# Attention pooling and a two-layer squared-ReLU block: a list planner with other durations, engine choice for the rounding, joined PSUM reads and 120-row token tiles

## The chip, the cores and the metric

The kernel runs on one core of a Trainium2 chip. The metric is device time in microseconds (us) of one execution; lower is better. A core has a matrix engine (PE, with its weight loads shown apart as PEld), a vector engine (DVE), a scalar engine (ACT), a general engine (POOL) and a queue engine (SP) that issues transfers. Each runs its own instruction list in order. A matrix product lands in PSUM, here eight banks of 512 float32 columns on 128 partitions; POOL doesn't read PSUM in this kernel.

## The reference

```python
def _attn_ref(x, inducing):            # x: 4 x 12480 x 128, inducing: 32 x 128
    ...
    def mab(q, kv):
        s = scale * (q @ kv.transpose(0, 2, 1))
        s = s - s.max(-1, keepdims=True)
        a = np.exp(s)
        a /= a.sum(-1, keepdims=True) + 1e-09
        return a @ kv
    h = mab(I, x)
    return mab(x, h)

def _moe_ref(x, w_in, w_out):          # 128 -> 2048 -> 128
    h = x @ w_in
    g = np.where(h >= 1, h, np.where(h <= -1, 0.0, (h + 1) ** 2 / 4))
    return g @ w_out
```

For each of four batches the 32 inducing rows attend over all 12480 tokens, then all tokens attend over the 32 summaries, and the 49920 results go through the two-layer block. The weights arrive as float64.

## The kernel before, in words

Tokens are cut into chunks of 480, 26 to a batch, 104 in all; four chunks are a group, seven groups a batch. Four kinds of work are listed as operations with an engine, a cost, a lag, a due time and buffers, and a planner sorts them:

- `load_in` and `load_out` fetch the weights in eight pieces each and turn float64 bits into float32 with six short DVE steps (`mag_bits`, `to_single`, `shift`, `upper`, `weight`, `lower`) and a POOL addition (`join`). A piece of `w_out` whose index is in `ROUND` is split into a rounded part `w_hi` and a rest `w_lo`; the other two stay whole (`w_f`).
- `summarize(b)` is the first attention. Per chunk it loads tokens as rows (`xn`: 96 partitions with 5 tokens each) and in columns (`xT`; in batch 0 by PE transposes and an ACT copy, L373, later by transfers and a DVE transpose, L388). Per group it makes scores (L407), maxima (L412), exponentials `e1` (ACT, L418), transposes them on PE (L439), copies them out to `eN` (L445, L446) and weighs the rows (L452). A chain `c1` to `c12` then folds the groups into `hT`, and `hw` is `hT` times the first weights (L556 to L566). So the first layer becomes one product of attention weights `aT` with `hw`.
- `attend(b, g)` is the second attention of a group: scores (L591), a DVE transpose, maximum, difference, exponential, sum (L614), the 1e-9 and the reciprocal (`invert`, L617 and L618), a product on POOL (`norm`), a transpose back, rounding on ACT and a rest on POOL (L632). Transfers then copy the result into `aT`. For the very first group POOL's two steps run on DVE (`hasty`).
- `chunk(b, c)` has eight steps k, 832 over the run, and is most of the work. Each step makes two products h (PE, L680), each with a bank of its own; two ACT instructions write max(h+1, 0) into the two halves of `w` (`rise`, L688, from here on the relu); one ACT instruction squares both halves (L695); two DVE instructions form min(max(h, 1), w) (`bound`, L701, the clamp). Six steps of eight are then rounded into `hi` (on the engine that `ROUND` names: four times DVE L716, once POOL L711, once ACT L713), POOL forms `lo = w - hi` (L719), and PE adds three products per half into the one bank `o` (L744). The other two steps add w in full float32. At a chunk's end DVE transposes `o` into `oT` (L754) and SP stores it.

The planner (`Plan.order`) walks time forward. When an engine is free it takes, among the operations whose inputs and buffers are ready by the listed costs and lags, the one with the earliest due time. Buffers are pools of slots (`SLOTS`): seven banks `h`, one bank `o`, eight `w`, four `hi`, four `lo`. A bank of the pool `h` is taken when a product is issued and given back after the clamp. The program that results is a fixed list per engine; on the chip semaphores alone decide when a row runs. So costs, lags and due times set the order and nothing else:

```python
ROUND = {0: "DVE", 1: "POOL", 3: "DVE", 4: "DVE", 6: "ACT", 7: "DVE"}
BEHIND = dict(h=-2600, r=-2000, s=-1000, t=0, hi=1200, lo=2400, p=7000, ps=12000)
...
if op.due < best.due:
```

Of the kernel before, what the change touches and what calls it, by code (L numbers as in the profile page):

```python
# [17 lines left out]
ROUND = {0: "DVE", 1: "POOL", 3: "DVE", 4: "DVE", 6: "ACT", 7: "DVE"}  # L18
# [6 lines left out]
BEHIND = dict(h=-2600, r=-2000, s=-1000, t=0, hi=1200, lo=2400, p=7000, ps=12000)  # L25

LEAD = 60000
# [5 lines left out]

class Slot:


    def __init__(self, pool, turn=None):
        self.pool, self.left, self.until, self.place, self.tile = pool, 0, 0, None, None
        self.turn = turn


class Op:


    def __init__(self, engine, cost, lag, due, emit, needs, uses):
        self.engine, self.cost, self.lag, self.due, self.emit = engine, cost, lag, due, emit
        self.uses = uses
        self.start = self.after = 0
        self.unmet, self.then = 0, []
        for n in needs:  # L50
            n.then.append(self)
            self.unmet += 1
        for s in self.uses:
            s.left += 1


class Plan:
# [5 lines left out]
    def add(self, engine, cost, lag, due, emit, needs=(), uses=()):  # L63
        op = Op(engine, cost, lag, due, emit, [n for n in needs if n], uses)
        self.ops.append(op)
        return op

    def order(self):
        engines = sorted({op.engine for op in self.ops})
        free = dict.fromkeys(engines, 0)  # L70
        able = {e: [] for e in engines}
        for op in self.ops:
            if not op.unmet:
                able[op.engine].append(op)
        spare = {p: [(0, i) for i in range(n)] for p, n in SLOTS.items()}
        turn = dict.fromkeys(SLOTS, 0)
        now, done = 0, []
        while len(done) < len(self.ops):
            later = []
            took = False  # L80
            for e in engines:
# [3 lines left out]
                best = None  # L85
                for op in able[e]:
                    at = op.after
                    opens = {}
                    for s in op.uses:
                        if s.place is None:  # L90
                            if s.turn not in (None, turn[s.pool]):
# [6 lines left out]
                    elif best is None or op.due < best.due:  # L98
                        best = op
# [3 lines left out]
                able[e].remove(best)  # L103
                best.start = now
                done.append(best)
                free[e] = now + best.cost
                later.append(free[e])
                for s in best.uses:
                    if s.place is None:
                        got = min(spare[s.pool])  # L110
                        spare[s.pool].remove(got)
                        s.place = got[1]
                        if s.turn is not None:
                            turn[s.pool] += 1
                seen = now + best.lag
                for s in best.uses:
                    s.left -= 1
                    s.until = max(s.until, seen)
                    if not s.left:
                        spare[s.pool].append((s.until, s.place))  # L120
                for n in best.then:
                    n.unmet -= 1
                    n.after = max(n.after, seen)
                    if not n.unmet:
                        able[n.engine].append(n)
# [7 lines left out]
def attn_moe(  # L133
# [14 lines left out]
    T = 5  # L148
    TP = 96
    CW = T * TP  # L150
    NB = CW // M
    R = TP // M
# [6 lines left out]
    assert NCH * CW == N and Q * M == P and C == P and R * M == TP and R * T == NB  # L159
# [6 lines left out]
    x_rows = x.rearrange("b (k p t) c -> b k p t c", p=TP, t=T)  # L166
# [4 lines left out]
        h=([P, 512], F32), o=([P, 512], F32), xn=([TP, T, C], F32), xT=([C, CW], F32),  # L171
        xr=([C, NB, M], F32), e1=([P, CW], F32), eN=([TP, T, P], F32), hw=([P, 512], F32R),
        w=([P, 2, CW], F32), hi=([P, 2, CW], F32R), lo=([P, 2, CW], F32R), aT=([P, CW], F32R),
        s2=([P, NB, M], F32), a=([P, CW], F32), ahi=([P, CW], F32R), oT=([C, NB, M], F32),
    )
    count = [0]

    def make(slot, shape=None, dtype=None):

        count[0] += 1  # L180
        where = psum if slot.pool in ("h", "o") else work
        s, d = FORM[slot.pool]
        slot.tile = where.tile(
# [12 lines left out]
    def in_turn(pool):  # L196
        turns[pool] += 1
        return Slot(pool, turns[pool] - 1)
# [46 lines left out]
    def load_f32(src, due, dst=None):  # L245
# [17 lines left out]

        def mag_bits():
# [5 lines left out]
        def to_single():  # L270

            nc.vector.tensor_scalar(
# [542 lines left out]
```

## Time and profile before

| what | value |
|---|---|
| median of 3 runs | 1832.63 us (1831.53 to 1833.14) |
| the profiled execution's own time | 1832.42 us |
| span in its trace | 1830.6 us |
| PE busy | 1736.9 us (95%) |
| DVE busy | 1714.6 us (94%) |
| ACT busy | 1724.2 us (94%) |
| POOL busy | 1579.0 us (86%) |

Around the span lie 1.8 us. Busy time counts an engine as busy while at least one instruction is under way, so with instructions that overlap in the pipeline a busy engine can still have room. What an instruction really costs in a full stretch is read from the distance of the starts in the timeline. PE's busy time has modelled ends. The share of 16 transfer engines in use is 0.28 by the page, so transfers don't fill theirs.

### The profile page before, as it was taken

What the parts mean: (1) busy time and instruction counts of PE and PEld (TensorE: products, weight loads), DVE (VectorE), ACT (ScalarE), POOL (GpSimd) and SP (SyncE); (2) the same over time, 40 slices, a digit from 0 to 9 for tenths busy, and PEclk for the clock granted to TensorE, in tenths of its full rate; (3) what the DMA queues carried; (4) which work ended last, traced back from release to release, by engine and by line L of the source; (5) the groups of instructions that cost most, each with busy time, mean ns of one, the idle gap of its engine ahead of it and who ended that gap; (6) DMA issues with size and microseconds to landing.
All of it is one profiled execution on the core that took longest, in us unless ns stands there. A gap on an engine that the chain in (4) does not pass through costs nothing.

```text
span 1830.6 us, 26794 instructions
## 1 busy us (share of the span) xinstructions
PE 1736.9 (95%) x8075; PEld 1235.7 (67%) x8075; DVE 1714.6 (94%) x2715; ACT 1724.2 (94%) x2807; POOL 1579.0 (86%) x810
## 2 busy tenths in 40 slices
PE   8699999999989999999999999999999999999998
PEld 5367767666667766767766766666676676677776
DVE  5999999999899999999999999999999999999997
ACT  7499999999989999999989999999998999999997
POOL 1499899888789989988978898898897999999997
PEclk9699999999999999999999999999999999999999
DMA  8532333222223333332223323332211111111111
GB/s 233 97 57 57 67 63 69 48 62 59 40 52 58 65 60 74 63 76 38 50 41 62 73 58 57 64 71 48 36 26 30 31 33 33 33 34 27 35 31 17
DMA packets 395200, 101.84 MB, mean 56 GB/s; under 512 B 369680, under 2 KB 383024, under 8 KB 395056
## 3 DMA queue, kind: packets, MB, share of 16 engines
q1 hardware_dynamic: 394960, 100.02, 28.1%
q8 instruction: 64, 1.05, 0.2%
q14 instruction: 80, 0.66, 0.1%
q10 hardware_dynamic: 96, 0.12, 0.0%
HBM read 48.94 MB, written 25.56 MB: 41 GB/s over the span
## 4 chain that ended last, share of the span: by engine, by line
PE 52%; ACT 21%; DVE 19%; issue 5%; DMA 1%; SPq 1%; POOL 0%; DVEq 0%; POOLq 0%; ACTq 0%
PE o L744 36%; PE h L680 10%; ACT w L688 10%; ACT w L695 9%; DVE w L701 8%; DVE hi L716 4%; DVE oT L754 3%; DVE sm L617 1%; PE h L452 1%; ACT hi L713 1%; PE h L591 1%; PE h L407 1%; PE h L439 1%; DMA xn<-in_x 1%; PE h L556 1%
## 5 line engine op out<-in xcount | busy, mean ns | idle before, releaser
L719 POOL TENSOR_TENSOR lo<-w,hi 128x960 fp32r<-128x960 f32 x624 | 1404.3, 2269 | 181.6 <-ACT hi L713 63.9
L701 DVE SCALAR_TENSOR_TENSOR w<-h,w 128x480 f32<-128x480 f32 x1664 | 991.8, 644 | 50.8 <-ACT w L695 48.8
L688 ACT ACTIVATE w<-h 128x480 f32<-128x480 f32 x1664 | 913.4, 627 | 50.8 <-PE h L680 48.1
L695 ACT ACTIVATE w<-w 128x960 f32<-128x960 f32 x832 | 888.2, 1068 | 3.0
L680 PE MATMUL h<-aT,hw 128*128 128x480 f32 x1664 | 639.1, 438 | 26.8 <-DVE w L701 10.1
L744 PE MATMUL o<-hi,w_hi 128*128 128x480 f32 x1248 | 496.6, 398 | 0.0
L716 DVE TENSOR_REDUCE hi<-w 128x960 fp32r<-128x960 f32 x416 | 472.1, 1135 | 16.6 <-PE o L744 1.6
L744 PE MATMUL o<-lo,w_hi 128*128 128x480 f32 x1248 | 473.5, 379 | 0.4 <-POOL lo L719 0.4
L744 PE MATMUL o<-hi,w_lo 128*128 128x480 f32 x1248 | 473.8, 380 | 0.0
L680 PEld LDWEIGHTS h<-aT,hw 128*128 128x128 f32 x1664 | 312.0, 189 | 210.2 <-DVE w L701 96.2
L744 PE MATMUL o<-w,w_f 128*128 128x480 f32 x832 | 388.2, 578 | 41.8 <-DVE oT L754 37.2
L744 PEld LDWEIGHTS o<-hi,w_hi 128*128 128x128 f32 x1248 | 234.5, 188 | 57.0 <-issue 25.1
L744 PEld LDWEIGHTS o<-hi,w_lo 128*128 128x128 f32 x1248 | 234.3, 188 | 46.9 <-issue 12.0
L744 PEld LDWEIGHTS o<-lo,w_hi 128*128 128x128 f32 x1248 | 234.1, 188 | 37.9 <-POOL lo L719 1.1
L744 PEld LDWEIGHTS o<-w,w_f 128*128 128x128 f32 x832 | 149.1, 190 | 161.5 <-issue 75.5
L713 ACT CAST hi<-w 128x960 fp32r<-128x960 f32 x104 | 107.2, 1031 | 5.2 <-DVE w L701 5.2
L711 POOL TENSOR_SCALAR hi<-w 128x960 fp32r<-128x960 f32 x104 | 104.4, 1004 | 0.0
L754 DVE STREAM_TRANSPOSE oT<-o 128x480 f32<-128x480 f32 x104 | 69.7, 670 | 8.9 <-PE o L744 7.6
L388 DVE STREAM_TRANSPOSE xT<-xr 128x480 f32<-128x480 f32 x78 | 51.8, 664 | 1.0 <-DMA xr<-in_x 1.0
L304 POOL TENSOR_TENSOR w_in_sb<-hi,lo 128x256 f32<-128x256 f32 x8 | 6.0, 755 | 36.3 <-DVE hi L294 36.3
L452 PE MATMUL h<-xn,eN 96*32 96x128 f32 x930 | 36.3, 275 | 0.5 <-ACT eN L445 0.5
L632 POOL TENSOR_TENSOR a<-a,ahi 128x480 fp32r<-128x480 f32 (+1 forms) x27 | 33.1, 1226 | 1.6 <-ACT ahi L629 1.6
(83 smaller groups left out, 616.8 us busy)
## 6 DMA issues: line engine op xcount, KB each, us to landing
out<-oT SPq DMA_DIRECT2D x416, 60.0 KB, 2.2
xn<-in_x SPq DMA_DIRECT2D x93, 240.0 KB, 3.9
xr<-in_x SPq DMA_DIRECT2D x312, 60.0 KB, 2.5
aT<-ahi SPq DMA_DIRECT2D x208, 60.0 KB, 2.0
aT<-a SPq DMA_DIRECT2D x206, 60.0 KB, 2.0
w<-in_x SPq DMA_DIRECT2D x11, 240.0 KB, 4.5
w<-in_moe_w_in SPq DMA_DIRECT2D x8, 256.0 KB, 5.3
w<-in_moe_w_out SPq DMA_DIRECT2D x8, 256.0 KB, 6.0
```

The costliest lines, as they stand in the source:

```text
L388: nc.vector.transpose(make(xT[b, c]), xr.tile.rearrange("c n i -> c (n i)"))
L452: nc.tensor.matmul(p[q * M : (q + 1) * M, :C], eN[g].tile[:, t, q * M : (q + 1) * M], xn[g * Q + q].tile[:, t, :], start=(t == 0), stop=(t ...
L680: nc.tensor.matmul(make(h)[:, :CW], hw[b][ft // 4].tile[:, ft % 4 * P : (ft % 4 + 1) * P], aT[b, c].tile, start=True, stop=True,)
L688: nc.scalar.activation(w.tile[:, i], h.tile[:, :CW], AF.Relu, bias=1.0)
L695: nc.scalar.activation(w.tile, w.tile, AF.Square, scale=0.5)
L701: nc.vector.scalar_tensor_tensor(w.tile[:, i], h.tile[:, :CW], 1.0, w.tile[:, i], op0=ALU.max, op1=ALU.min)
L711: nc.gpsimd.tensor_scalar(make(hi), w.tile, 1.0, 0.0, op0=ALU.mult, op1=ALU.add)
L713: nc.scalar.copy(make(hi), w.tile)
L716: nc.vector.tensor_reduce(make(hi), w.tile.unsqueeze(3), axis=AX.X, op=ALU.max)
L719: nc.gpsimd.tensor_sub(make(lo), w.tile, hi.tile.bitcast(F32))
L744: nc.tensor.matmul(acc.tile[:, :CW], wt, g, start=(first and n == 0), stop=(last and n == len(terms) - 1),)
L754: nc.vector.transpose(make(oT).rearrange("c n i -> c (n i)"), acc.tile[:, :CW])
```

## The change

- The planner's costs and lags are replaced by other numbers, and it knows three more things: on the same engine a result is usable a fixed time (`RAW`) after the cost; an operation may list several engines with a cost, lag and due time for each; and PE pays `RETILE` when it changes between products that use the whole array and products that use part of it. `KEEP` is 0, so that last rule doesn't move the choice.
- The rounding into `hi` lists DVE, ACT and POOL, with later due times for ACT and POOL, in place of a fixed engine for each k. The batches' `eN` copies list DVE and ACT.
- All eight banks are one PSUM tile, `banks`, and a slot is a number in it. If the two products of a step stand in an even bank and the next, and both are ready, the two relus become one instruction over 960 columns, and likewise the two clamps.
- Batches 1 to 3 load rows as 4 tokens for each of 120 partitions, 480 pieces of 512 bytes in place of 96 of 2560, so the exponentials are transposed in 4 pieces, not 5, fill one bank, and one copy makes `eN`. `e1` and `xT` are written in order and read in strides, where before both the read and the write were strided.
- `to_single` and `join` of `w_out` run on POOL, `join` of `w_in` on DVE; the middle of the `w_out` conversion waits for batch 0's `hT`, and `load_out` is listed after `summarize(0)`.
- The 1e-9 of `attend` moves from DVE to POOL (`guard`).
- Of the three terms of a split product, the one with `w_lo` is issued first.

In the program that comes out, 169 of 832 relu pairs and 249 of 832 clamp pairs are joined. Roundings on DVE go from 416 to 384, on ACT from 104 to 99, on POOL from 104 to 141. DVE has 18 full `eN` copies less of each of two kinds and 10 of the new kind; ACT has 8 of the new kind more. Products in the weighing step go from 520 to 442. POOL gains 28 guards.

The core of the diff:

```diff
-ROUND = {0: "DVE", 1: "POOL", 3: "DVE", 4: "DVE", 6: "ACT", 7: "DVE"}
+SPLIT = (0, 1, 3, 4, 6, 7)
...
-BEHIND = dict(h=-2600, r=-2000, s=-1000, t=0, hi=1200, lo=2400, p=7000, ps=12000)
+BEHIND = {
+    "h": -4400, "r": -3050, "s": -500, "t": 400, "hi": 3300, "hi ACT": 1900, "hi POOL": 9600,
+    "lo": 2200, "p": 9300, "ps": 8900,
+}
+RAW = dict(DVE=205, ACT=130, POOL=100, PE=100, SP=0)
...
+    def pick(self, spare, now):
+        free = {i for t, i in spare if t <= now}
+        if self.near and self.near.place is not None and self.near.place ^ 1 in free:
+            return self.near.place ^ 1
+        if self.first:
+            return min(free, key=lambda i: (i ^ 1 not in free, i % 2, i))
+        return min(free, key=lambda i: (i ^ 1 in free, i))
...
+    def beside(self):
+        a, b = self.uses[0].place, self.twin.uses[0].place
+        return a % 2 == 0 and b == a + 1
...
+                if best.merged and best.beside():
+                    other = best.twin
+                    if other in able[e] and other.ready(e) <= now:
...
-    x_rows = x.rearrange("b (k p t) c -> b k p t c", p=TP, t=T)
+    x_rows = x.rearrange("b (k t p) c -> b k p t c", p=120, t=4)
...
+        spare = nc.vector if first else nc.gpsimd
...
-        v = add("DVE", 340, 470, due, upper, [v], [raw, top])
+        v = add("DVE", 360, 500, due, upper, [v, after], [raw, top])
...
+        def guard():
+            nc.gpsimd.tensor_scalar(sm[:rows], sm[:rows], 1e-9, None, op0=ALU.add)
         def invert():
-            nc.vector.tensor_scalar(sm[:rows], sm[:rows], 1e-9, None, op0=ALU.add)
             nc.vector.reciprocal(sm[:rows], sm[:rows])
...
+    def each(of, i, hs_, w, do):
+        if of[1 - i].wide:
+            return
+        if of[i].wide:
+            do(w.tile, banks[:, hs_[0].place : hs_[0].place + 2, :CW])
+        else:
+            do(w.tile[:, i], hs_[i].tile[:, :CW])
...
-                u = add(ROUND[k], cost, lag, due + BEHIND["hi"], upper, ts, [hi, w])
+                ways = dict(
+                    DVE=(1058, 1285, at), ACT=(884, 1065, at + BEHIND["hi ACT"]),
+                    POOL=(1085, 1180, at + BEHIND["hi POOL"]),
+                )
+                u = add(ways, 0, 0, at, lambda upper=upper, by=by: upper(by=by), ts, [hi, w])
...
                         terms = [
+                            (w_lo[k][:, i, :], hi.tile[:, i, :]),
                             (w_hi[k][:, i, :], hi.tile[:, i, :]),
-                            (w_lo[k][:, i, :], hi.tile[:, i, :]),
                             (w_hi[k][:, i, :], lo.tile[:, i, :]),
```

DVE in the start, from the first step of batch 0's chain (`m_0`, L489 before and L568 after, is `c1`). Before, conversions of `w_out` (L266 to L294) stand between the steps of the chain:

```order
L489 TENSOR_REDUCE m_0_94<-mg 128x1
L283 SCALAR_TENSOR_TENSOR lo_898<-w_802,lo_898 128x256
L266 TENSOR_SCALAR hi_910<-w_811 128x256
L495 TENSOR_REDUCE mrow_95<-h_907 1x128
L289 TENSOR_SCALAR hi_889<-lo_898 128x256
L272 TENSOR_SCALAR hi_910<-hi_910 128x256
L294 SCALAR_TENSOR_TENSOR hi_889<-w_802,hi_889 128x256
L507 TENSOR_SCALAR nm_96<-h_916 128x1
```

The same place after:

```order
L568 TENSOR_REDUCE m_0_81<-mg 128x1
L574 TENSOR_REDUCE mrow_82<-banks 1x128
L586 TENSOR_SCALAR nm_83<-banks 128x1
L592 TENSOR_TENSOR fs_84<-banks,sg 128x7
L593 TENSOR_REDUCE tot_85<-fs_84 128x1
L599 TENSOR_SCALAR rs_86<-banks 128x1
L600 RECIPROCAL rs_86<-rs_86 128x1
L603 SCALAR_TENSOR_TENSOR ff<-banks,rs_86,fold 128x224
L615 COPY hT_859<-banks 128x128
L351 SCALAR_TENSOR_TENSOR lo_775<-w_652,lo_775 128x256
```

The conversions moved behind `hT` (L536 before, L615 after).

DVE at the end of a chunk in the middle of the run, from the transpose of `o`. Before, clamps are 480 wide, one by one (L701), and L716 is the rounding:

```order
L754 STREAM_TRANSPOSE oT_8451<-o_8235 128x480
L716 TENSOR_REDUCE hi_8455<-w_8387 128x960
L701 SCALAR_TENSOR_TENSOR w_8418<-h_8392,w_8418 128x480
L701 SCALAR_TENSOR_TENSOR w_8418<-h_8412,w_8418 128x480
L701 SCALAR_TENSOR_TENSOR w_8435<-h_8416,w_8435 128x480
L716 TENSOR_REDUCE hi_8482<-w_8418 128x960
L701 SCALAR_TENSOR_TENSOR w_8435<-h_8422,w_8435 128x480
```

After, at the same transpose (L855; L788 is the clamp, L811 the rounding):

```order
L855 STREAM_TRANSPOSE oT_7384<-banks 128x480
L788 SCALAR_TENSOR_TENSOR w_7323<-banks,w_7323 128x480
L811 TENSOR_REDUCE hi_7396<-w_7309 128x960
L788 SCALAR_TENSOR_TENSOR w_7369<-banks,w_7369 128x960
L788 SCALAR_TENSOR_TENSOR w_7388<-banks,w_7388 128x480 x2
L788 SCALAR_TENSOR_TENSOR w_7398<-banks,w_7398 128x480 x2
L811 TENSOR_REDUCE hi_7443<-w_7388 128x960
L811 TENSOR_REDUCE hi_7452<-w_7398 128x960
```

One clamp of this piece is joined, and roundings stand further behind their clamps.

POOL in the first chunks, where L711 (after: L806) is a rounding and L719 (after: L814) forms `lo`. Before, a rounding stands ahead of its own `lo`, once in eight steps:

```order
L711 TENSOR_SCALAR hi_1499<-w_1427 128x960
L719 TENSOR_TENSOR lo_1510<-w_1427,hi_1499 128x960
L719 TENSOR_TENSOR lo_1534<-w_1459,hi_1519 128x960
L719 TENSOR_TENSOR lo_1566<-w_1479,hi_1549 128x960
L719 TENSOR_TENSOR lo_1594<-w_1517,hi_1582 128x960
L719 TENSOR_TENSOR lo_1617<-w_1538,hi_1602 128x960
```

After:

```order
L806 TENSOR_SCALAR hi_1389<-w_1322 128x960
L806 TENSOR_SCALAR hi_1403<-w_1338 128x960
L814 TENSOR_TENSOR lo_1415<-w_1322,hi_1389 128x960
L814 TENSOR_TENSOR lo_1440<-w_1338,hi_1403 128x960
L806 TENSOR_SCALAR hi_1462<-w_1393 128x960
L814 TENSOR_TENSOR lo_1476<-w_1374,hi_1449 128x960
```

Roundings come in bunches there, and a `lo` of an older step can stand behind a rounding of a newer one.

More of the change, by code (lines that the diff above doesn't have):

```diff
@@ L102, in order @@
                 took = True
[L103 to L107, printed above, removed]
+                for x in best.choice:
+                    able[x].remove(best)
+                cost, lag, _ = best.choice[e]
                 for s in best.uses:
                     if s.place is None:
[L110 to L114, printed above, removed]
@@ L115, in order @@
-                seen = now + best.lag
-                for s in best.uses:
+                        s.place = s.pick(spare[s.pool], now)
+                        spare[s.pool] = [x for x in spare[s.pool] if x[1] != s.place]
+                        turn[s.pool] += s.turn is not None
+                both = [best]
+                if best.merged and best.beside():
+                    other = best.twin
+                    if other in able[e] and other.ready(e) <= now:
+                        able[e].remove(other)
+                        both.append(other)
+                        best.wide = True
+                        cost, lag = best.merged
@@ L117, in order @@
+                if e == "PE" and best.tiled != tiled:
+                    cost, lag, tiled = cost + RETILE, lag + RETILE, best.tiled
+                for op in both:
+                    op.start, op.engine, op.cost, op.lag = now, e, 0, lag
+                    done.append(op)
+                best.cost = cost
+                free[e] = now + cost
+                later.append(free[e])
+                for s in [s for op in both for s in op.uses]:
                     s.left -= 1
-                    s.until = max(s.until, seen)
+                    s.until = max(s.until, now + lag)
@@ L175, in attn_moe @@
     )
+    banks = psum.tile([P, SLOTS["h"] + SLOTS["o"], 512], F32, name="banks")
     count = [0]
@@ L180, in make @@
         count[0] += 1
-        where = psum if slot.pool in ("h", "o") else work
+        if slot.pool in ("h", "o"):
+            slot.tile = banks[:, slot.place + (SLOTS["h"] if slot.pool == "o" else 0), :]
+            return slot.tile
         s, d = FORM[slot.pool]
-        slot.tile = where.tile(
+        slot.tile = work.tile(
             shape or s, dtype or d, tag=f"{slot.pool}{slot.place}", name=f"{slot.pool}_{count[0]}"
@@ L672, in chunk, with square @@
             w = in_turn("w")
[L673 to L676 removed]
+            h0 = in_turn("h")
+            hs_ = [h0, in_turn("h", h0)]
+            ms, rs_, ts = [], [], []
+            def square(w=w):
+                nc.scalar.activation(w.tile, w.tile, AF.Square, scale=0.5)
+            for i, h in enumerate(hs_):
                 def hidden(k=k, i=i, h=h):
@@ L694, in square @@
-            def square(w=w):
-                nc.scalar.activation(w.tile, w.tile, AF.Square, scale=0.5)
-            s = add("ACT", 896, 1036, due + BEHIND["s"], square, ss, [w])
-            for i in range(2):
-                def bound(i=i, h=hs_[i], w=w):
-                    nc.vector.scalar_tensor_tensor(
-                        w.tile[:, i], h.tile[:, :CW], 1.0, w.tile[:, i], op0=ALU.max, op1=ALU.min
-                    )
-                ts.append(add("DVE", 565, 700, due + BEHIND["t"] + i, bound, [s], [hs_[i], w]))
```

223 lines of the change are left out of this document (134 added, 89 removed).

## Prediction

> **What bounds the kernel now.** I read, in this order, busy time by stretch, the chain of work that ended last, the waits, and the timeline for the distance of starts. First the page's span and the stretch from 77 us (just after the first relu) to the last transpose; its columns are start and end, length, then busy time (and count) of PE, PEld, DVE, ACT, POOL, then clock, share of transfers and GB/s. Then the chain from 120 to 1790 us by engine and line.
>
> ```profile
> span 1830.6 us, 26794 instructions
> 77.00:1825.00 1748.00, 1683.95 (x7545) 1202.01 (x7544) 1661.97 (x2568) 1681.36 (x2731) 1561.20 (x783) 1.00 0.27 50
> by line: PE o L744 38.1%; PE h L680 10.6%; ACT w L688 10.4%; ACT w L695 9.5%; DVE w L701 8.5%; issue 5.4%; DVE hi L716 4.1%; DVE oT L754 2.7%; DVE sm L617 1.3%; ACT hi L713 1.2%; PE h L591 1.1%; PE h L452 1.1%; PE h L407 0.7%; PE h L439 0.5
> ```
>
> No engine bounds this alone. In 1748 us PE idles 64, ACT 67, DVE 86, POOL 187, and the chain passes through PE, ACT and DVE in turn. POOL hardly stands in it. The clock is full. What costs time is that in-order engines wait for each other; who waits for DVE says most (idle of PE before h and before o, us and times, and the two rows of ACT and DVE):
>
> ```profile
>   DVE w L701: 106.3, 323
>   DVE oT L754: 48.9, 92
>   POOL lo L719: 1.5, 3
> ACT w L688 <- PE h L680: 48.1, 76, 1.7
> DVE w L701 <- ACT w L695: 48.8, 102, 1.5
> L719 POOL TENSOR_TENSOR lo<-w,hi 128x960 fp32r<-128x960 f32 x624 | 1404.3, 2269 | 181.6 <-ACT hi L713 63.9 <-DVE hi L716 61.1 <-PE h L680 19.8
> ```
>
> PE waits 106.3 us for clamps to give banks back and 48.9 us for `o` to be transposed, 155 us of waiting for DVE (loads and products both counted). Then ACT waits 48.1 us for PE's h. For `lo` PE waits only 1.5 us: POOL's 181.6 us of idle are slack today.
>
> **The change part by part.** True prices, from distances of starts (start, length, engine, instructions):
>
> ```profile
> 1019.18 1.08 ACT L688 ACTIVATE w<-h 128x480 f32<-128x480 f32 x2
> 1020.08 1.08 ACT L695 ACTIVATE w<-w 128x960 f32<-128x960 f32 x1
> 1020.98 1.10 ACT L688 ACTIVATE w<-h 128x480 f32<-128x480 f32 x2
> 1028.62 1.14 ACT L713 CAST hi<-w 128x960 fp32r<-128x960 f32 x1
> 1029.50 1.17 ACT L695 ACTIVATE w<-w 128x960 f32<-128x960 f32 x1
> 1023.80 1.78 DVE L701 SCALAR_TENSOR_TENSOR w<-h,w 128x480 f32<-128x480 f32 x3
> 1025.49 1.14 DVE L716 TENSOR_REDUCE hi<-w 128x960 fp32r<-128x960 f32 x1
> 1026.55 3.12 DVE L701 SCALAR_TENSOR_TENSOR w<-h,w 128x480 f32<-128x480 f32 x5
> 1004.21 0.99 POOL L711 TENSOR_SCALAR hi<-w 128x960 fp32r<-128x960 f32 x1
> 1005.17 1.21 POOL L632 TENSOR_TENSOR a<-a,ahi 128x480 fp32r<-128x480 f32 x1
> ```
>
> A relu pair takes 0.90, a square 0.90, an ACT rounding 0.88; three clamps take 1.69, so a pair 1.13; a DVE rounding 1.06, a POOL rounding 0.96.
>
> *DVE's load.* 32 roundings fewer: 32 x 1.06 = 34 us. Joined clamps: no such instruction ran; the nearest of 960 columns is the rounding, 1.06, so 249 x (1.13 - 1.06) = 17 us (bounds: 0, and 249 x 0.56 = 139 if the second half cost nothing, which the equal ACT rows for 2 x 480 and 960 columns speak against). For the guard and `eN`, and for what else is priced below:
>
> ```profile
> L617 DVE TENSOR_SCALAR sm<-sm x28: 160/916/2090, 68.6 to 1742.5; 128x15 f32<-128x15 f32 x24, 64x15 f32<-64x15 f32 x4
> L617 DVE TENSOR_SCALAR sm<-sm 128x15 f32<-128x15 f32 x24 | 24.4, 1018 | 0.0
> L445 DVE COPY eN<-h 96x512 f32<-96x512 f32 x18 | 12.1, 675 | 0.0
> L446 DVE COPY eN<-h 96x128 f32<-96x128 f32 x18 | 4.9, 275 | 0.0
> L418 ACT ACTIVATE e<-h,nb 128x480 f32<-128x480 f32 x24 | 22.9, 954 | 0.0
> L611 ACT ACTIVATE s<-s 128x480 f32<-128x480 f32 x24 | 15.2, 634 | 3.0 <-DVE s L606 3.0
> L373 ACT COPY xT<-h 128x480 f32<-128x480 f32 x26 | 24.8, 1071 | 6.9 <-PE h L368 6.9
> L629 ACT CAST ahi<-a 128x480 fp32r<-128x480 f32 x24 | 15.4, 643 | 0.3 <-DVE a L626 0.3
> L452 PE MATMUL h<-xn,eN 96*32 96x128 f32 x930 | 36.3, 275 | 0.5 <-ACT eN L445 0.5
> L439 PE MATMUL h<-ident,e 128*96 128x128 f32 x120 | 17.9, 276 | 3.1 <-DVE w L701 2.2 <-ACT e L418 0.7
> ```
>
> The guard touches 15 columns and takes 0.16 to 2.09 us: a fixed small work and a stall up to the length of one POOL `lo` (2.27). Off DVE it frees some 27 us, and by the chain (1.3% of 1670) 22 of them lie on the path. On POOL it costs 28 x 0.16 = 4 us. `eN` gives back 12.1 + 4.9 - 10 x 0.675 = 10 us, with the half-sized copies some 12. Together 34 + 17 + 27 + 12 = 90 us, and DVE's busy time falls from 1662 to 1572.
>
> *What that is worth.* At least the 22 us on the chain, at most all 90. Between them I scale PE's wait with DVE's ratio of busy to idle time, an assumption of mine and not a reading: 1662/86 = 19 before; with a stretch of some 1700, 1572/128 = 12, a third less. A third of PE's 155 us is **52 us**, my value; it lies between the ends, and the row it rests on (106.3 and 48.9) is the wait that I think ends last.
>
> *ACT.* 5 roundings fewer: -4. Joined relus: 169 x (0.90 - 0.90) is 0 by the nearest row, the square; at most 169 x 0.45 = 76, for which nothing speaks; I take 0. 8 `eN` copies more, at DVE's 0.675: +5. The exponentials L418 lose one strided side: between 0 and 21 x (0.954 - 0.634) = 7; half, -3. Net **-2**.
>
> *PE.* For 21 groups 4 of 20 weighing products and one of 5 transposes go: 78 products are two records each, 36.3/930 x 2 x 78 = 6, and 21 x 17.9/120 = 3. Half of PE's time is on the chain: **-4**. `w_lo` first issues the same products: 0, since its third term still waits for `lo`, as before. One `banks` tile: dependences still go by bank: 0.
>
> *POOL.* 37 roundings x 0.96 = 36, guards 4, so 40 us more; today they would fit into 187 us of idle. But a rounding ahead of a `lo` makes that one 0.96 later, and behind `lo` wait PE's products, the `hi` and `lo` slots and the end of the chunk. From 0 (hidden) to 40; a third, **+13**, since idle shrinks to about 100.
>
> *Start.* The last copy of a group's sum (a row of the timeline), then pieces of the chain (start, length, what):
>
> ```profile
> 48.44 0.25 ACT L459 COPY hs<-h 64x128 f32<-64x128 f32 x1
> 50.50 0.15 DVE m L489
> 50.98 0.73 DVE hi L266
> 53.34 0.73 DVE hi L266
> 54.67 0.73 DVE hi L272
> 59.57 0.30 DVE hT L536
> 79.41 0.64 DVE w L701
> ```
>
> `c1` starts 1.8 us after its last input (48.69), and three conversions of 0.73 stand in the chain to `hT`: up to 1.8 + 2.2 = 4 us earlier without them. `xT` copies become like L629: 26 x (1.071 - 0.643) = 11 us less ACT work in the start, of which I count 3, as PE and transfers alternate with ACT there. But the conversions come back between `hT` and the first clamp, where DVE is busy: some 15 more of 0.2 to 0.3 us, +4, against attention steps of later groups put off. Net **-3**, between -9 and +4. On POOL `to_single` and `join` meet an idle engine there.
>
> *Transfers.* 480 pieces per chunk of rows:
>
> ```profile
> xn<-in_x SPq DMA_DIRECT2D x93, 240.0 KB, 3.9
> xr<-in_x SPq DMA_DIRECT2D x312, 60.0 KB, 2.5
> ```
>
> `xr` moves 480 small pieces in 2.5 us already. Even if 78 loads took twice 3.9 us each, nine slots and a group per 3.3 chunks (over 50 us) cover them; without that cover it would be 78 x 3.9 = 304 us. SP has the same 1263 issues: 0.
>
> *Sum.* 1830.6 - 52 - 2 - 4 + 13 - 3 = 1782.6 us of span; with the 1.8 us around it 1784.4, and the median shown lies 0.2 above the profiled execution's 1832.42: **1784.6**.
>
> The Trainium skill, "Perfetto Trace Analysis", section "Optimizing Scalar/DVE Operations", gives a DVE instruction about 125 ns of fixed access time on PSUM and an ACT one about 51 ns. By that, an estimate from that page, joined clamps would save 31 us, not 17, and joined relus 9, not 0, and the sum would be some 15 us lower. The two equal ACT rows here (0.90) disagree for ACT, and the sum stays with them.
>
> **Rivals.**
> - *More gain (about 1759).* ACT's own work by starts is 832 x 1.80 + 104 x 0.88 = 1590 and some 55 of smaller things, 1645 in 1748. If the new order keeps ACT at 98% of its starts, the stretch is about 1677 ((1645 - 2)/0.98), the span 1830.6 - 71 - 3, and 2 around it: 1758.6. For it: all waits named above end at DVE. Against: PE, ACT and POOL would all be above 95%.
> - *Waits move (about 1815).* Only the chain's 22 us come back, ACT, PE and the start give 9, and POOL takes 13: 1830.6 - 18 + 1.8. For it: ACT and PE were as idle as 67 and 64 us, so something else may end next.
> - *Joining holds banks (about 1810).* A joined clamp gives its first bank back 0.56 us later. PE waited before 323 of 1664 products; 249 x 0.56 x 323/1664 = 27 us. The same section says that breaking instructions up may let work finish sooner where the engine isn't full but makes others idle, which is this rule against the change; the trace shows the bank wait but no joined instruction.
> - *POOL decides, slower (about 1870).* If POOL's idle time isn't slack but the latency of rounding into `lo`, it stays: 1561 + 40 + 187 = 1788 in place of 1748, +40, less 3. For it: POOL's idle ends 61.1 us at DVE's and 63.9 at ACT's rounding, and bunched POOL roundings lengthen that way. Against: only 1.5 us of PE's waits end at `lo`. It decides once POOL's idle stays above some 150 us.
> - *No change (1829 to 1836).* The order is no better in sum: the later due times of the rounding eat what DVE gives.
>
> **Chances.** Forecast (1765 to 1804) 0.45, more gain 0.13, waits move 0.16, joining 0.09, POOL slower 0.12, no change 0.05. A measurement of this kernel tells some 0.2% (about 4 us) from no change. Faster 0.83, same 0.05, slower 0.12. The range 1748 to 1828 leaves out the slower cases and the low tail.
>
> **What would show it.** Right: DVE's busy time 1600 to 1640 us in all, waits of PE's h for the clamp near 70 us and of o for the transpose near 35, the guard at about 0.2 us on POOL or stalled there at no one's cost, POOL's idle before `lo` near 100. A joined clamp's start-to-start distance of 1.06, a joined relu's 0.90. `hT` at 55 to 56 us and the first clamp at 75 to 79. Wrong: PE waiting tens of us for `lo` (POOL), unchanged waits for clamps with 960-wide clamps ending them (joining), or ACT idle before h unchanged.

## The result and the profile after

The changed kernel takes 1785.14 us (median of 4 runs, 1782.57 to 1786.76) beside 1832.42 for the kernel before: a ratio of 0.9741, 95% interval 0.9724 to 0.9758, or 47.5 us less. The forecast was 1784.6. Executions at a lower clock are left out of all ratios: one of the four of s6 below (3136.64 us at a granted clock of 0.83) and one of the kernel before (1940.1 us at 0.85).

The total came out as forecast, but not by the route it was given. First the page's span and busy times, then the stretch from 70 us to the last transpose (start and end, length, busy time of PE, PEld, DVE, ACT, POOL, clock, transfers, GB/s; the first relu is at 75.7):

```profile
span 1784.7 us, 25996 instructions
PE 1718.4 (96%) x7898; PEld 1231.5 (69%) x7898; DVE 1636.2 (92%) x2376; ACT 1693.5 (95%) x2642; POOL 1619.7 (91%) x875
70.00:1779.00 1709.00, 1665.80 (x7373) 1197.51 (x7369) 1596.58 (x2263) 1663.93 (x2572) 1611.35 (x860) 0.99 0.28 52
```

In this stretch PE idles 43 us, ACT 45, POOL 98 and DVE 112 (before, in 1748 us: 64, 67, 187, 86). DVE now has more slack than POOL. The waits (who waits, for whom: us, times, longest) and the group of `lo`:

```profile
PEld banks L775 <- DVE w L788: 98.3, 255, 4.7
PE banks L775 <- DVE w L788: 14.6, 18, 4.2
PEld banks L845 <- DVE oT L855: 33.2, 66, 1.3
PE banks L845 <- DVE oT L855: 13.8, 32, 1.2
PEld banks L845 <- ACT w L783: 7.5, 13, 1.6
PEld banks L845 <- ACT w L769: 5.8, 14, 0.6
PEld banks L845 <- POOL lo L814: 3.3, 6, 1.1
ACT w L783 <- PE banks L775: 21.2, 36, 1.5
L814 POOL TENSOR_TENSOR lo<-w,hi 128x960 fp32r<-128x960 f32 x624 | 1400.0, 2271 | 68.9 <-DVE hi L811 22.5 <-ACT hi L808 12.6 <-PE banks L775 9.0
```

PE's waits for clamps are 112.9 us (106.3 before) and for the transposed `o` 47.0 (48.9 before). The waits that the forecast cut by a third did not fall. These two rows of the kernel before did, from 66.7 us to the 13.3 of the fifth and sixth row above:

```profile
PEld o L744 <- ACT w L688: 42.9, 53, 1.8
PEld o L744 <- ACT w L695: 23.8, 35, 2.2
```

The stretch from the first clamp to the last one is 50 us shorter; the start, up to the first clamp, is 4.5 us longer. The clamp's line in the changed kernel, then in the kernel before:

```profile
L788 DVE SCALAR_TENSOR_TENSOR w<-banks,w x1415: 586/647/1159, 83.9 to 1772.2; 128x480 f32<-128x480 f32 x144, 128x960 f32<-128x960 f32 x33
```

```profile
L701 DVE SCALAR_TENSOR_TENSOR w<-h,w x1664: 584/646/664, 79.4 to 1818.0; 128x480 f32<-128x480 f32 x185
```

(The columns are shortest, median and longest duration in ns, then first and last start: 1688.3 us between these in the changed kernel, 1738.6 before.) Of the 50 us between these two starts, 31 are idle time of PE (62.5 before, 31.3 after) and 19 its busy time (1676.1 before, 1657.0 after, with modelled ends). So PE's idle time alone cannot have given the 52 us that the forecast took from it.

Joined instructions as the timeline has them (start, length; the distance to the next start is the price), first DVE, then ACT:

```profile
620.59 1.15 DVE L788 SCALAR_TENSOR_TENSOR w<-banks,w 128x960 f32<-128x960 f32 x1
621.65 0.67 DVE L855 STREAM_TRANSPOSE oT<-banks 128x480 f32<-128x480 f32 x1
656.02 1.00 ACT L783 ACTIVATE w<-banks 128x960 f32<-128x960 f32 x1
656.88 1.03 ACT L769 ACTIVATE w<-w 128x960 f32<-128x960 f32 x1
```

A joined clamp costs 1.06 us, as estimated; a joined relu costs 0.86, where the forecast had 0.90, the price of two single ones.

### The profile page after: what moved, and what is told of

Its sections match the earlier page's. It is cut to its first block, busy times and chain, and to the rows that moved or that the text cites. A ratio compares the mean times of both kernels' runs of the same rounds, so it can differ in the third digit from the quotient of the medians.

```text
span 1784.7 us, 25996 instructions
## 1 busy us (share of the span) xinstructions
PE 1718.4 (96%) x7898; PEld 1231.5 (69%) x7898; DVE 1636.2 (92%) x2376; ACT 1693.5 (95%) x2642; POOL 1619.7 (91%) x875
## 4 chain that ended last, share of the span: by engine, by line
PE 58%; ACT 17%; DVE 14%; issue 5%; POOL 2%; DMA 2%; SPq 1%; DVEq 0%; POOLq 0%; ACTq 0%
PE banks L845 41%; PE banks L775 12%; ACT w L783 9%; DVE w L788 7%; ACT w L769 7%; DVE hi L811 2%; DVE oT L855 2%; POOL lo L814 2%; PE banks L670 1%; PE banks L531 1%; PE banks L478 1%; DMA xr<-in_x 1%; ACT hi L808 1%; DMA xn<-in_x 1%; PE banks L635 1%
## 5 line engine op out<-in xcount | busy, mean ns | idle before, releaser
L814 POOL TENSOR_TENSOR lo<-w,hi 128x960 fp32r<-128x960 f32 x624 | 1400.0, 2271 | 68.9 <-DVE hi L811 22.5
L788 DVE SCALAR_TENSOR_TENSOR w<-banks,w 128x480 f32<-128x480 f32 (+1 forms) x1415 | 977.3, 732 | 72.7 <-ACT w L769 61.5
L783 ACT ACTIVATE w<-banks 128x480 f32<-128x480 f32 (+1 forms) x1495 | 874.6, 649 | 23.3 <-PE banks L775 21.2
L775 PE MATMUL banks<-aT,hw 128*128 128x480 f32 x1664 | 580.5, 427 | 24.4 <-DVE w L788 14.6
L845 PE MATMUL banks<-hi,w_lo 128*128 128x480 f32 x1248 | 541.5, 434 | 17.8 <-DVE oT L855 13.8
L845 PE MATMUL banks<-lo,w_hi 128*128 128x480 f32 x1248 | 474.9, 381 | 0.8 <-POOL lo L814 0.7
L845 PE MATMUL banks<-hi,w_hi 128*128 128x480 f32 x1248 | 474.0, 380 | 0.0
L811 DVE TENSOR_REDUCE hi<-w 128x960 fp32r<-128x960 f32 x384 | 435.9, 1139 | 15.8 <-PE banks L845 1.1
L775 PEld LDWEIGHTS banks<-aT,hw 128*128 128x128 f32 x1664 | 305.9, 189 | 179.5 <-DVE w L788 98.3
L845 PE MATMUL banks<-w,w_f 128*128 128x480 f32 x832 | 390.9, 566 | 0.0
L845 PEld LDWEIGHTS banks<-hi,w_lo 128*128 128x128 f32 x1248 | 235.1, 188 | 131.6 <-issue 54.1
L845 PEld LDWEIGHTS banks<-hi,w_hi 128*128 128x128 f32 x1248 | 235.3, 189 | 59.9 <-issue 30.9
L806 POOL TENSOR_SCALAR hi<-w 128x960 fp32r<-128x960 f32 x141 | 140.7, 1002 | 12.6 <-DVE w L788 5.8
L855 DVE STREAM_TRANSPOSE oT<-banks 128x480 f32<-128x480 f32 x104 | 70.1, 674 | 8.4 <-PE banks L845 7.6
L340 POOL TENSOR_SCALAR hi<-hi 128x256 f32<-128x256 f32 x8 | 9.1, 1140 | 46.9 <-DVE hi L334 46.6
```

The source lines that it names most:

```text
L775: nc.tensor.matmul(make(h)[:, :CW], hw[b][ft // 4].tile[:, ft % 4 * P : (ft % 4 + 1) * P], aT[b, c].tile, start=True, stop=True,)
L783: each(of, i, hs_, w, lambda to, h: nc.scalar.activation(to, h, AF.Relu, bias=1.0))
L788: lambda to, h: nc.vector.scalar_tensor_tensor(to, h, 1.0, to, op0=ALU.max, op1=ALU.min),
L806: nc.gpsimd.tensor_scalar(make(hi), w.tile, 1.0, 0.0, op0=ALU.mult, op1=ALU.add)
L811: nc.vector.tensor_reduce(make(hi), w.tile.unsqueeze(3), axis=AX.X, op=ALU.max)
L814: nc.gpsimd.tensor_sub(make(lo), w.tile, hi.tile.bitcast(F32))
```

## The experiments

Two theories explain the 47 us. The *load theory* is the forecast's: DVE has less to do, so it answers PE sooner. The *order theory* says that the new due times (later for clamp, rounding and unsplit products, earlier for h, relu and split products) put PE's work where its inputs are ready. For single parts there are rivals of their own. Since the kernels ran on more than one chip, the differences below are differences of ratios to the kernel before on the same chip, times 1832.4 us; each is uncertain by some 4 us.

The table collects all runs. The last columns are the sum of PE's waits in the trace by the engine waited for (loads and products both counted, so a sum is more than PE's idle time), and busy times.

| kernel | median us | ratio (95%) | PE waits for DVE | for ACT | for POOL | DVE busy | ACT busy |
|---|---|---|---|---|---|---|---|
| before | 1832.42 | 1 | 219 | 84 | 3 | 1714.6 | 1724.2 |
| after | 1785.14 | 0.9741 (0.9724 to 0.9758) | 211 | 25 | 4 | 1636.2 | 1693.5 |
| s4, before with the new due times | 1824.15 | 0.9946 (0.993 to 0.9963) | 291 | 20 | 4 | 1707.2 | 1718.3 |
| s5, after with the old due times | 1848.25 | 1.0086 (1.0071 to 1.0101) | 277 | 54 | 17 | 1582.8 | 1773.8 |
| s10, s5 with the engines' offsets kept | 1823.28 | 0.9943 (0.9928 to 0.9957) | 243 | 53 | 9 | 1620.7 | 1735.2 |
| s13, before without the 1e-9 | 1810.59 | 0.9872 (0.9855 to 0.989) | 178 | 88 | 3 | 1687.1 | 1721.0 |
| s3, before with the 1e-9 on POOL | 1844.76 | 1.0066 (1.0051 to 1.0081) | 245 | 85 | 3 | 1687.7 | 1727.1 |
| s1, after with the 1e-9 on DVE | 1799.62 | 0.9821 (0.9806 to 0.9835) | 244 | 26 | 5 | 1659.1 | 1697.4 |
| s2, after with joined work split | 1794.72 | 0.9789 (0.9772 to 0.9805) | 223 | 26 | 4 | 1651.5 | 1703.3 |
| s6, after with fixed engines | 1809.3 | 0.9867 (0.985 to 0.9883) | 256 | 24 | 6 | 1670.6 | 1701.8 |
| s11, s6 with after's totals | 1809.20 | 0.9864 (0.9848 to 0.9879) | 254 | 21 | 15 | 1638.8 | 1696.7 |
| s12, after with another lead | 1787.72 | 0.9748 (0.9732 to 0.9763) | 220 | 24 | 3 | 1629.4 | 1694.1 |
| s7, after with 96 x 5 rows | 1806.92 | 0.9853 (0.9837 to 0.9869) | 221 | 22 | 8 | 1628.7 | 1704.2 |
| s8, after with the old conversion | 1777.33 | 0.969 (0.9676 to 0.9705) | 203 | 27 | 6 | 1634.7 | 1694.7 |

**s4: the new due times alone, in the kernel before**

```diff
-BEHIND = dict(h=-2600, r=-2000, s=-1000, t=0, hi=1200, lo=2400, p=7000, ps=12000)
+BEHIND = dict(h=-4400, r=-3050, s=-500, t=400, hi=3300, lo=2200, p=9300, ps=8900)
-LEAD = 60000
+LEAD = 66950
```

> The kernel before (its costs, fixed engines, single instructions, 96-row tiles, guard on DVE) with the due times and the lead of the changed kernel, planned anew. Order theory (due times are what matters): much of the gain, 1795 to 1815 us, with DVE as loaded as before. Load theory (the new due times only pay once DVE is relieved): 1825 to 1845.

9.9 us less. That lies between the two ranges, far from the order theory's: the due times alone do not carry the gain. The waits of PE's h and o:

```profile
PEld h L680 <- DVE w L701: 164.3, 489, 1.9
PE h L680 <- DVE w L701: 13.7, 30, 1.1
PEld o L744 <- DVE oT L754: 50.7, 102, 2.4
PE o L744 <- DVE oT L754: 10.0, 13, 2.1
PEld o L744 <- ACT w L688: 7.1, 24, 0.8
PEld o L744 <- ACT w L695: 3.2, 15, 0.2
```

The due times turn waits for ACT into waits for DVE: `o` no longer waits for relus and squares (66.7 to 10.3 us), but h, asked for earlier, waits 178.0 us for clamps in place of 106.3. This is the base from which the relief has to be read: 178.0 + 60.7 = 239 us here, 160 in the changed kernel.

**s5 and s10: the old due times, in the changed kernel**

```diff
-    "h": -4400, "r": -3050, "s": -500, "t": 400, "hi": 3300, "hi ACT": 1900, "hi POOL": 9600,
-    "lo": 2200, "p": 9300, "ps": 8900,
+    "h": -2600, "r": -2000, "s": -1000, "t": 0, "hi": 1200, "hi ACT": 0, "hi POOL": 0,
+    "lo": 2400, "p": 7000, "ps": 12000,
-LEAD = 66950
+LEAD = 60000
```

> The changed kernel with the due times of the kernel before (and its lead of the attention), planned anew; costs, engine choice, joining, tiles stay. Load theory: DVE's load stays low, so most of the gain stays, 1785 to 1800 us. Order theory: the due times are what matters, 1810 to 1830 us, with PE's waits at the full float32 products back near 70 us.

Slower than the kernel before, which neither size foresaw. The edit had also taken the offsets `hi ACT` and `hi POOL`, and the planner then gave ACT 202 roundings, DVE 303 and POOL 119. The page's busy times:

```profile
PE 1750.3 (95%) x7898; PEld 1223.4 (66%) x7898; DVE 1582.8 (86%) x2422; ACT 1773.8 (96%) x2796; POOL 1601.9 (87%) x853
```

DVE has 53 us less to do than in the changed kernel, ACT 80 more, and the time is 63 us longer. s10 is the same with `"hi ACT": 1900, "hi POOL": 9600` kept, and the choice came out as 157, 357 and 110:

> As the run with the old due times (1848 us, where 202 roundings went to ACT), but with the changed kernel's extra due time for rounding on ACT and POOL kept; now 157 roundings are on ACT, 357 on DVE, 110 on POOL. ACT-load theory (that run was slow because ACT got 103 x 0.88 = 91 us more): 58 x 0.88 = 51 us more on ACT give some 35 us, 1815 to 1825. Order theory (the old due times let banks wait however the work is spread): 1840 to 1850.

37 us more than the changed kernel with 42 us more on ACT. PE's waits for ACT are 53 to 54 us in both (25 in the changed kernel). Between s5 and s10, 39 us of ACT's load go with 26 us of time, while DVE has 38 us more to do in the faster one: this fits load at ACT being dear here and load at DVE not. The way is not PE's own wait for ACT, which stays, but DVE's wait for ACT's squares (148.8 us in s5, 84.5 in s10, 61.5 in the changed kernel) and PE's wait for DVE behind it. How much of the remaining 37 us is order and how much load, these two do not separate.

**s13: the kernel before, the 1e-9 left out**

```diff
-            nc.vector.tensor_scalar(sm[:rows], sm[:rows], 1e-9, None, op0=ALU.add)
             nc.vector.reciprocal(sm[:rows], sm[:rows])
```

> The kernel before in its own order with the 1e-9 of the second attention left out (the sums there are at least 1). It shows what the guard's stall cost without a new wait for POOL. Prediction's step (22 us of the guard on the chain): 1808 to 1812 us. If another wait takes its place, as where the guard went to POOL in this order: 1822 to 1832.

23.5 us less. The chain's 1.3% of 1670 us, 22 us, was a true price. The waits of h for the clamp fell from 106.3 to 85.9:

```profile
PEld h L679 <- DVE w L700: 80.3, 252, 1.5
PE h L679 <- DVE w L700: 5.6, 15, 1.1
```

What the additions stall on can be read in the kernel before. One of the longest stands beside a `lo` of POOL, and both end together (358.81 + 2.08 and 358.63 + 2.23); the third row is one that meets no POOL instruction:

```profile
358.81 2.08 DVE L617 TENSOR_SCALAR sm<-sm 128x15 f32<-128x15 f32 x1
358.63 2.23 POOL L719 TENSOR_TENSOR lo<-w,hi 128x960 fp32r<-128x960 f32 x1 [0.67 <-PE h L680]
603.86 0.16 DVE L617 TENSOR_SCALAR sm<-sm 128x15 f32<-128x15 f32 x1
```

Of the 28 additions, 25 end 0.02 to 0.04 us after a POOL instruction that was under way when they started. The other three meet none and take 0.16 to 0.17 us.

**s3: the kernel before, the 1e-9 on POOL, same order**

```diff
-            nc.vector.tensor_scalar(sm[:rows], sm[:rows], 1e-9, None, op0=ALU.add)
+            nc.gpsimd.tensor_scalar(sm[:rows], sm[:rows], 1e-9, None, op0=ALU.add)
```

> The kernel before in its own order, with only the 1e-9 of the second attention moved to POOL. Load theory: the 22 us that the guard had on the chain come back, 1806 to 1811 us. Order theory: another wait takes its place, 1825 to 1832; a guard queued behind two or three POOL instructions could make the reciprocal on DVE wait and cost up to 10 us more.

Slower by 12 us. On POOL the 28 additions take 0.26 us each, but they stand in its queue behind a `lo`, and DVE's reciprocal, with clamps behind it, waits for them:

```profile
L617 POOL TENSOR_SCALAR sm<-sm x28: 252/258/263, 67.4 to 1755.1; 128x15 f32<-128x15 f32 x24, 64x15 f32<-64x15 f32 x4
```

```profile
DVE sm L618 <- POOL sm L617: 39.7, 27, 2.7
```

Against s13, where nothing waits, that is 36 us, near the 39.7 of the wait. So the move alone loses, and only a plan that gives POOL time for it and puts other work ahead of the reciprocal wins. In the changed kernel the wait is 2.8 us:

```profile
L696 POOL TENSOR_SCALAR sm<-sm 128x15 f32<-128x15 f32 x24 | 6.2, 260 | 9.8 <-PE banks L845 4.6 <-DVE sm L693 3.3 <-PE banks L775 0.2
L699 DVE RECIPROCAL sm<-sm 128x15 f32<-128x15 f32 x24 | 5.6, 233 | 3.0 <-POOL sm L696 2.8
```

**s1: the changed kernel, the 1e-9 back on DVE, same order**

```diff
         def guard():
-            nc.gpsimd.tensor_scalar(sm[:rows], sm[:rows], 1e-9, None, op0=ALU.add)
+            pass
         def invert():
+            nc.vector.tensor_scalar(sm[:rows], sm[:rows], 1e-9, None, op0=ALU.add)
             nc.vector.reciprocal(sm[:rows], sm[:rows])
```

> The changed kernel with every instruction in its place, but the 1e-9 of the second attention is added on DVE again (28 instructions, before the reciprocal). Load theory (the gain is work taken off DVE, the guard's stall behind POOL above all): some 22 to 27 us slower than the changed kernel, 1807 to 1812 us, with the guard near 1 us each on DVE. Order theory (the gain is the new order, engines have room): DVE's stall is absorbed, less than 8 us slower, 1785 to 1793.

14.7 us more, less than the 23.5 of the kernel before: between the ranges of the two theories. The additions stall there as they did before:

```profile
L699 DVE TENSOR_SCALAR sm<-sm x28: 129/674/2125, 65.7 to 1706.0; 128x15 f32<-128x15 f32 x24, 64x15 f32<-64x15 f32 x4
```

**s2: each joined relu and clamp issued as two halves, same order**

```diff
-            do(w.tile, banks[:, hs_[0].place : hs_[0].place + 2, :CW])
+            for j in range(2):
+                do(w.tile[:, j], hs_[j].tile[:, :CW])
```

> The changed kernel in the same order, but each joined relu or clamp is issued as its two halves at the same place (169 and 249 more instructions). Load theory: DVE gets 249 x 0.07 = 17 us more, of which some 10 reach the time, 1795 us. Holding theory (a joined clamp gives its first bank back 0.56 us late): up to 27 us faster, 1758 to 1780. Order theory: within 4 us of 1785.

8.8 us more, near the 10 of the load theory. DVE is busy 15.3 us longer and ACT 9.8. If joining held banks, the halves would have freed PE; its waits for clamps go from 112.9 to 117.8:

```profile
PEld banks L776 <- DVE w L789: 106.2, 290, 4.2
PE banks L776 <- DVE w L789: 11.6, 14, 3.7
```

**s6, s11 and s12: the planner's choice of engine**

s6 gives each rounding of the changed kernel the engine of the old table and plans anew (416 on DVE, 104 on ACT, 104 on POOL):

```diff
+                e = {0: "DVE", 1: "POOL", 3: "DVE", 4: "DVE", 6: "ACT", 7: "DVE"}[k]
+                ways = {e: (ways[e][0], ways[e][1], at)}
                 u = add(ways, 0, 0, at,
```

> The changed kernel with the rounding on the engine that the old table fixes for each k (416 on DVE, 104 on ACT, 104 on POOL), planned anew, all else as changed. If the free choice carries the gain: DVE gets 32 x 1.06 = 34 us back and POOL's bunches go, 1810 to 1825 us. If order and the other reliefs carry it: 1780 to 1795.

23.1 us more. Is that DVE's 32 extra roundings, or the freedom? s11 keeps engines fixed but with the totals of the changed kernel, 384, 99 and 141:

```diff
+                n = b * NCH + c
+                if k == 4 and n * 37 // 104 != (n + 1) * 37 // 104:
+                    e = "POOL"
+                if k == 6 and n * 5 // 104 != (n + 1) * 5 // 104:
+                    e = "DVE"
```

> The changed kernel with fixed engines for the rounding again, but in 37 chunks the fifth step's rounding goes to POOL and in 5 chunks the seventh step's to DVE, so that the totals are those of the changed kernel (384 DVE, 99 ACT, 141 POOL). Load theory (the 25 us that fixed engines cost are DVE's 34 us): 1785 to 1795 us. Freedom theory (it matters that the engine is free at that moment): 1803 to 1815 us.

22.5 us more, though DVE's busy time is the changed kernel's within 3 us. So DVE's total is not what the fixed table costs. s11 and s6 differ by 0.6 us, with 32 roundings less on DVE, 5 less on ACT and 37 more on POOL: taking the 34 us off DVE gains nothing that can be seen when POOL gets them by a fixed table (PE's waits for POOL go from 6 to 15 us). The free choice is worth some 22 us. Both runs also leave out the later due times that go with the choice (`hi ACT` and `hi POOL`), and between s5 and s10 these two alone moved the time by 26 us. How much of the 22 is the freedom to take the engine that is free at that moment, and how much these due times, no run separates. The waits of s11:

```profile
PEld banks L775 <- DVE w L788: 134.1, 356, 4.7
PE banks L775 <- DVE w L788: 18.9, 33, 4.2
DVE w L788 <- ACT w L769: 88.3, 150, 2.7
PEld banks L852 <- POOL lo L814: 12.4, 34, 1.0
```

DVE waits 88.3 us for squares (61.5 in the changed kernel), and PE 153.0 for clamps (112.9). In s11 DVE has the time, but not when it is needed. In s6, which is as slow, DVE waits only 62.8 us for squares; what the two share is PE's wait for DVE, 256 and 254 us in place of 211.

Planning anew could shift the time by itself. s12 changes one number that should not matter, `LEAD = 66950` to `66000`:

> The changed kernel with the attention's lead at 66000 in place of 66950, an edit that means nothing by itself but makes the planner write another order. It shows how far re-planning alone moves the time. If plans differ little: 1782 to 1788 us. If they scatter: 5 to 15 us away, and the replanned comparisons of this study are no finer than that.

1.3 us more, though 154 relus are joined there in place of 169 and 273 clamps in place of 249. That is one other plan only, but it speaks for taking the 20 us and more of s6, s7 and s11 as effects.

**s7: tiles of 96 rows of 5 tokens in all batches**

```diff
-    SHAPE = [(5, 96)] + [(4, 120)] * (B - 1)
+    SHAPE = [(5, 96)] * B
```

(with the copies into two banks, the fifth transpose and the old costs of `eN` that belong to it)

> The changed kernel with rows of 96 x 5 tokens in all batches (5 transposes, 2 copies and 20 weighing products per group again), planned anew. Load theory: DVE, ACT and PE get 12, 4 and 9 us of work back; some 4 to 12 us slower, 1789 to 1797 us. If the tiles don't matter: within 4 us of 1785.

20.5 us more, where this expectation had 4 to 12 and the forecast some 10. The page's busy times:

```profile
PE 1730.4 (96%) x8075; PEld 1236.9 (69%) x8075; DVE 1628.7 (90%) x2377; ACT 1704.2 (94%) x2685; POOL 1624.6 (90%) x880
```

PE has 12.0 us more to do and ACT 10.7, and PE's waits for DVE grow by 10 us. DVE has 7.5 us less to do, not 12 more, since the plan gave it 12 roundings fewer and ACT 7 more. Which of these carries the 20 is open.

**s8: the weights converted on the engines and in the order of before**

```diff
-        side, one, two = ("DVE", 205, 340) if first else ("POOL", 330, 680)
+        side, one, two = "POOL", 205, 700
-        v = add(side, one, one + 130, due, to_single, [v], [mag])
-        v = add("DVE", 360, 500, due, upper, [v, after], [raw, top])
+        v = add("DVE", one, one + 130, due, to_single, [v], [mag])
+        v = add("DVE", 360, 500, due, upper, [v], [raw, top])
...
+    for k in range(NP):
+        load_out(k, -29000 + 2500 * k)
...
-            for k in range(NP):
-                load_out(k, -16000 + 2500 * k)
```

(and `to_single` of both weights on DVE, `join` of both on POOL)

> The changed kernel with the second weights converted as before: DVE and POOL share the steps in the old way, nothing waits for the first batch's summary, listed and due early. The start theory (the new conversion costs the start 4.6 us: first clamp at 84.0 us against 79.4): first clamp near 79 us and 1780 us, unless the new plan's main loop differs by some us either way. Rival (the start is set by the attention of the first group): first clamp stays at 83 to 84.

9.3 us less than the changed kernel: the best version, ahead of both. Some 6.7 of it is the start; the rest is no more than what a measurement and another plan can differ by. The first step of batch 0's chain, `hT` and the first clamp (pieces of the chain, then the line's row):

```profile
48.99 0.08 DVE m L567
57.49 0.30 DVE hT L614
```

```profile
L787 DVE SCALAR_TENSOR_TENSOR w<-banks,w x1452: 587/648/1162, 77.2 to 1761.4; 128x480 f32<-128x480 f32 x156, 128x960 f32<-128x960 f32 x26
```

The first clamp is at 77.2 in place of 83.9. In the changed kernel `hT` and the first clamp stand here:

```profile
59.81 0.30 DVE hT L615
83.98 1.07 DVE w L788
```

So 2.3 of the 6.7 us lie before `hT` and 4.4 behind it. DVE ahead of batch 0's chain in the changed kernel:

```profile
49.00 0.29 DVE L334 TENSOR_SCALAR hi<-w 128x256 uint32<-128x256 uint32 x1 [0.54 <-DMA w<-in_moe_w_out]
50.21 0.38 DVE L334 TENSOR_SCALAR hi<-w 128x256 uint32<-128x256 uint32 x1 [0.92 <-DMA w<-in_moe_w_out]
50.51 0.27 DVE L345 TENSOR_SCALAR lo<-hi 128x256 uint32<-128x256 uint32 x1
51.77 0.29 DVE L345 TENSOR_SCALAR lo<-hi 128x256 uint32<-128x256 uint32 x1 [0.99 <-POOL hi L340]
51.98 0.15 DVE L568 TENSOR_REDUCE m<-mg 128x1 f32<-128x7 f32 x1
```

Only the middle of the conversion was made to wait for `hT`. Its first steps still stand ahead of batch 0's chain (L568), and there DVE waits twice for a load and once for POOL's `to_single` (L340), 2.5 us in these five rows. On POOL that step lasts 1.14 us (its row below); in the kernel before, on DVE, it took 0.39 on the mean. The first step of the chain starts at 52.0 us, in s8 at 48.9 and in the kernel before at 50.5.

```profile
L340 POOL TENSOR_SCALAR hi<-hi 128x256 f32<-128x256 f32 x8 | 9.1, 1140 | 46.9 <-DVE hi L334 46.6
```

Behind `hT` follow the steps that were put off until then. Between `hT` and the first clamp DVE runs 28 conversion steps in the changed kernel, 17 in s8 and 13 in the kernel before, and they take some 12, 5 and 5 us of its queue, waits for POOL included. ACT is held up as well:

```profile
79.02 0.41 ACT L406 CAST w_hi<-hi 128x256 fp32r<-128x256 f32 x1 [2.24 <-POOL hi L369]
80.25 1.00 ACT L769 ACTIVATE w<-w 128x960 f32<-128x960 f32 x1
```

The first relu runs early (at 75.7 us, in the kernel before at 77.0), but in ACT's queue the first square stands behind a step of the conversion that waits 2.24 us for POOL. The square ends at 81.25, and its clamp waits another 2.7 us in DVE's queue, behind the last of the 28 steps and two transposes of `xT`. Which part of s8's edit (the engine of a step, the place in the list or the wait for `hT`) gives how much was not tried.

## Why the prediction came out right, point by point

- **The guard, 22 us on the path: right.** s13 gives 23.5, and the stall on POOL's `lo` that the forecast read from the durations stands in the trace. The forecast did not ask what POOL's queue would do to the reciprocal behind it; s3 shows 12 us of loss in place of a gain where the order isn't planned for it. In the changed kernel its return costs 14.7.
- **Joined clamps, 17 us of DVE by 1.06 each: right.** s2 gives 15.3 of busy time. In time, these and the relus' 9.8 us on ACT give 8.8 together.
- **Joined relus, 0: mis-sized.** They save 0.04 us each, 9.8 us of ACT in s2. The Trainium skill, "Perfetto Trace Analysis", section "Optimizing Scalar/DVE Operations", led to an estimate of 9 for ACT and 31 for DVE: ACT's busy time agrees, DVE's is half of it.
- **"A third of PE's waits for DVE", 52 us: the sum is near, the step failed.** In the profile the waits went from 155.2 to 159.9 us, not to 104. The forecast held the order still, and the order moved: in s4 the due times alone bring these waits to 238.7, and from there to the changed kernel they fall by 33%. The waits that went are PE's for ACT before `o`, which the forecast had not looked at. The third is an agreement in number: of the 90 us that it was worked out from, the 34 of the roundings gave nothing that can be seen as load (s6 beside s11). What the roundings gave was the free choice with its due times, 22 us, which no term of the sum had.
- **Tiles: mis-sized.** The forecast had 12 us of DVE and 9 of PE work, 5 of ACT against them, some 10 us of time; s7 gives 20.5, with PE's part of the work at 12.0.
- **PE, -4: the size in time stays open.** Its busy time fell by 18.5 us (1736.9 to 1718.4, with modelled ends), where the forecast had 9.
- **ACT, -2: mis-sized.** Its busy time fell by 30.7 us. The exponentials and the `xT` copies gave more than was counted: 954 to 694 ns and 1071 to 563. The forecast, and the text on the change, had it that one of two strided sides goes. In the code of the kernel before (L373 and L418) the read is in order and only the write is strided; the change moves the strides from the write to the read. The rows after:

```profile
L444 ACT COPY xT<-banks 128x480 f32<-128x480 f32 x26 | 14.0, 563 | 10.9 <-PE banks L439 10.8
L495 ACT ACTIVATE e<-banks,nb 128x480 f32<-128x480 f32 x24 | 16.7, 694 | 3.0 <-DVE nb L486 3.0
```

- **POOL, +13: not seen.** Its 40 us of more work came as forecast (1579.0 to 1619.7 busy), its idle before `lo` fell from 181.6 to 68.9 (forecast near 100), and PE's waits for `lo` stayed small, 4.2 us (1.5 before). The slack was slack, and the rival that ends slower falls with it. With fixed engines (s11) these waits are 12.4 for the loads alone.
- **The start, -3: wrong in sign.** It got 4.5 us longer. The part that was to bring 4 us brought none: three conversion steps left the chain to `hT`, but others stayed ahead of it, waited for loads and for POOL and let it start 1.5 us later, so `hT` came at 59.8 us (59.6 before, 55 to 56 forecast). POOL was idle there, as the forecast said, but three times as slow at the step, and DVE, in order, waited for it. The part that was to cost 4 us cost more: behind `hT` stand 15 more steps, as forecast, but at some 7 us of DVE's queue, not 4, and they hold up ACT too. s8 takes back 6.7.
- **Rivals.** "More gain" asked for 1677 us from the first relu to the last transpose; it took some 1703. "Joining holds banks" falls in s2, "POOL decides" by the waits. "Waits move" was half right: the due times moved them from ACT to DVE (s4), and the rest of the change then took as much away again. "No change" is s4's case but for 10 us: the due times without the rest.

The errors went in opposite directions: the start came out 7.5 us worse than forecast and the choice of engine was missing as a gain, while POOL's 13 us of loss were not there and the main term took credit for roundings that as load gave nothing and cut waits that did not fall. That the total was met to 1 us is chance; of the main term's parts, the runs bear out the guard and the joined clamps.

What the parts are worth inside the changed kernel is 14.7 (guard), 8.8 (joining), 22.5 (choice of engine), 20.5 (tiles) and -9.3 (conversion), 57 in sum beside a gain of 47.5. They overlap, and the due times cannot be taken out alone, since they also steer the choice. No run takes back the planner's new costs and lags with `RAW`, the place of the `w_lo` term, or the strides of `e1` and `xT` by themselves; what these are worth in time is not shown.

## What to carry to other kernels

When a change reorders a program and lightens an engine as well, read the waits against a kernel with the new order alone; against the old one the same relief looked like nothing. Here the planner's free choice of engine, with its due times, was worth 22 us where the totals per engine alone gave 0.6; so before a load relief is priced, ask whether the engine is late because it is full or because it is asked at the wrong time. A small instruction goes to another engine only with a place in that engine's queue: the same move lost 12 us unplanned and won 15 planned.

## What the runs showed of the hardware

- The addition of 1e-9 on 15 columns took 0.13 to 2.13 us on DVE and 0.25 to 0.27 on POOL. In the kernel before, 25 of 28 on DVE end 0.02 to 0.04 us after a POOL instruction that was under way when they started, so they stalled until it ended; the longest is near one POOL `lo` (2.27). The Trainium skill, "SBUF — State Buffer", section "Who interferes with whom", says that a DVE `tensor_scalar` can need the port pair that it shares with GpSimd and then waits for the whole of the other's instruction; these common ends agree. That the port is the reason is not shown by them.
- An ACT copy of 480 columns out of PSUM took 1071 ns when it read in order and wrote in strides, and 563 when it read in strides and wrote in order. The exponentials went from 954 to 694 ns with the same exchange.
- Joining two PSUM reads of 480 columns saves 0.07 us of a clamp's 1.13 on DVE and 0.04 of a relu's 0.90 on ACT, by the distance of starts.
